# Gate parts brought to the scores' left factor by DMA, first choice's marks in PSUM, constants two units earlier

## The chip, the cores and the metric

The kernel runs on one core of one Trainium2 chip. The metric is the device time of one execution in microseconds (us). Beside the median of three runs there is one profiled execution, from which all rows below come. Engine names in rows: PE is TensorE's matmul, PEld its weight load, DVE VectorE, ACT ScalarE, POOL GpSimd, and SPq the queue of SyncE, which issues nearly all transfers here.

## The reference

A recurrent attention, then a mixture of experts with a capacity, then a dense MLP. The change touches the attention and the first step of the assignment.

```python
for t in range(S):                       # q, k, v: 4 batches x 8 heads x 768 x 40
    m_new = np.maximum(f[t] + m, i[t])
    f_stab, i_stab = np.exp(f[t] + m - m_new), np.exp(i[t] - m_new)
    C = f_stab * C + i_stab * outer(v[t], k[t]); n = f_stab * n + i_stab * k[t]
    y[t] = sigmoid(o[t]) * (C @ q[t]) / np.maximum(abs(n @ q[t]), 1.0)
logits = x @ w_gate                      # 3072 tokens x 8 experts, from the reshaped y
# tokens go to experts in order of falling logit, at most 384 to one expert
out = expert MLP of each token's expert, then a dense MLP of all tokens
```

## The kernel before

The sequence is cut into 9 chunks of 86 steps (`NCH`, `L`). A unit is one chunk `c` of one batch `b` with its 8 heads; the loop in `attention` runs over 36 units `u`, and `score(u)` runs two units ahead of `value(u)`. Within a chunk the recurrence is a matrix of scores: `pS` is keys by queries, `W` is the exponential of a sum of gate terms, `dk` their product, and `pY` the product of `dk` with the values.

The exponent is itself a matmul. `pE` = `cE`^T `aE`: the gate sums of a key position (`cp`, its input part) and those of a query position (`ap`) are each split into three bfloat16 parts, and `cE` (left factor) and `aE` (right factor) hold these parts beside constant rows of ones, of an identity and of the mask. There are three buffers of each, used in turn by `c % 3`. `gates` computes `cp` and `ap` with one partition for each of the 32 pairs, which lie (batch, head): partition 8b + h. Its three generators cover chunk 0, chunks 1 to 3 and chunks 4 to 8.

- `load_a(c)` brings `ap` to three rows of `aE` with three DMAs, for chunk c + 2 in the unit with b = 3 of chunk c, behind `load_qk` and `load_k` of that chunk in the same queue.
- `gates_rows(c)` brings `cp` to 24 rows of `cE`: 12 matmuls with a 0/1 matrix `sel` put the parts into PSUM (`pc`), ScalarE copies them to `cE`. It is called in the unit with b = 2, for chunk c + 1.

In the code's order SP's queue gets, per chunk: in b = 2 `load_v(c + 2)` and `load_o(c + 1)`; in b = 3 `load_qk` (two `q`, one `k`), `load_k` (`kr`), `load_a` (three `aE`); in each unit from u = 8 on the next half of the dense MLP's 64-bit weights (`words`, tile `r`), which `float32_of` turns into float32 on ACT, DVE and POOL, one half in two units up to u = 23 and one in each from u = 24; and in each unit the store `xd` of unit u - 2. `rows` splits loads and stores of 86 rows into 80 and 6.

`first_choice` finds each token's best expert from transposed logits, at units 25 (four chunks), 33 (three), 37 and at the end (one each): the logits `lg` lie in the PSUM tile `pT` (32 columns for a token, 8 of them used), the marks `ch` in the SBUF tile `fc`. `constants` is a generator of eight steps, `cst`: ten small loads on SP in the first three, then small tables by GpSimd and VectorE. One step is taken per unit from u = 28:

```python
if u >= 28:
    next(cst, None)
```

After the loop come `store_logits`, the assignment (`rounds`) beside the rest of the conversion, and the MLPs; nothing in them is touched.

Of the kernel before, what the change touches and what calls it, by code (L numbers as in the profile page):

```python
# [9 lines left out]
F32 = mybir.dt.float32  # L10
F32R = mybir.dt.float32r
BF = mybir.dt.bfloat16
# [4 lines left out]
OP = mybir.AluOpType  # L17
AX = mybir.AxisListType

B, H, S, D = 4, 8, 768, 40  # L20
DM = H * D
N = B * S
E = 8
CAP = N // E
L = 86
NCH = 9
SP = L * NCH
X = D + L
KE = 27 + L
# [8 lines left out]
OUT = 1.0e38  # L38
# [22 lines left out]
def host_constants():  # L61
    import ml_dtypes
    bf = ml_dtypes.bfloat16
    ce = np.zeros((KE, X), np.float32)
    ce[24:27, :] = 1.0
    ce[27:, :L] = np.eye(L)
    ae = np.zeros((KE, H, L), np.float32)
    for p in range(3):
        for h in range(H):
            ae[p * 8 + h, h, :] = 1.0  # L70
    ae[27:] = np.where(np.arange(L)[:, None] > np.arange(L)[None, :], -1e30, 0.0)[:, None, :]
    sel = np.zeros((32, B, 3, 24), np.float32)
    for b in range(B):
        for p in range(3):
            for h in range(H):
                sel[8 * b + h, b, p, 8 * p + h] = 1.0
    g = np.arange(128)
    return {
        "c_blk": (g[:, None] // 16 == g[None, :] // 16).astype(bf),
        "c_pre": ((g[:, None] // 16 == g[None, :] // 16) & (g[:, None] < g[None, :])).astype(bf),  # L80
        "c_tri": (g[:, None] < g[None, :]).astype(bf),
        "c_sel": sel.astype(bf),
        **steps(""), **steps("_a"),
        "c_ce": np.pad(ce, ((0, 128 - KE), (0, 0))).astype(bf),
        "c_ae": np.pad(ae.reshape(KE, H * L), ((0, 128 - KE), (0, 0))).astype(bf),
    }


def host_layout(inp):
    q, k, v = inp["q"], inp["k"], inp["v"]  # L90
    o = {}

    def chunks(a):
        p = np.zeros((B, H, SP, a.shape[-1]), np.float32)
        p[:, :, :S] = a
        return p.reshape(B, H, NCH, L, a.shape[-1])

    def dmajor(a):
        a = chunks(a).reshape(B, 4, 2, NCH, L, D).transpose(3, 2, 5, 0, 1, 4)
        return np.ascontiguousarray(a).reshape(NCH, 2, D, 16, L)  # L100

    def rows(a):
        return np.ascontiguousarray(chunks(a).transpose(2, 3, 0, 1, 4))

    o["h_q"] = dmajor(q)
    o["h_kt"] = dmajor(k).reshape(NCH, 2 * D, 16, L)
    o["h_kr"] = rows(k).reshape(NCH, L, 32, D)
    ve = np.ones((NCH, L, 32, D + 1), np.float32)
    ve[..., :D] = rows(v).reshape(NCH, L, 32, D)
    o["h_v"] = ve  # L110
    o["h_o"] = rows(inp["o_gate"]).reshape(NCH, L, B, DM)
    o["h_i"] = np.ascontiguousarray(inp["i_gate"].reshape(32, S))
    o["h_f"] = np.ascontiguousarray(inp["f_gate"].reshape(32, S))
    wg = np.zeros((128, 3, 32), np.float32)
    for d in range(3):
        n = min(128, DM - 128 * d)
        wg[:n, d, :E] = inp["moe_w_gate"][128 * d:128 * d + n]
    o["h_wg"] = wg

    def dblocks(w):  # L120
        f = w.shape[-1] // 128
        a = np.concatenate([w[..., :DM, :], w[..., 256:DM, :]], axis=-2)
        a = a.reshape(w.shape[:-2] + (3, 128, f, 128))
        return np.moveaxis(a, (-4, -3, -2, -1), (-2, -3, -4, -1))

    we = np.empty((E, FE, 128, 2, 384), np.float32)
    we[:, :, :, 0] = dblocks(inp["moe_w1"]).reshape(E, FE, 128, 384)
    w2 = inp["moe_w2"].reshape(E, FE, 128, DM)
    we[:, :, :, 1, :64] = w2[..., 256:]
    we[:, :, :, 1, 64:] = w2  # L130
    o["h_we"] = we.reshape(E, FE, 128, 768)
    wf = np.empty((NF, 128, 384 + DM), np.int64)
    wf[:, :, :384] = dblocks(np.ascontiguousarray(inp["moe2_w_in"]).view(np.int64)).reshape(NF, 128, 384)
    wf[:, :, 384:] = np.ascontiguousarray(inp["moe2_w_out"]).view(np.int64).reshape(NF, 128, DM)
    o["h_wf"] = wf
    o["h_al"] = np.ascontiguousarray(inp["moe2_alpha"].reshape(NF, 128).T)
    o.update(host_constants())
    return o

# [20 lines left out]
class Kern:  # L160
# [80 lines left out]
    def gates_setup(self, p):  # L241
        nc, a = self.nc, self.a
        self.gp = p
        P = 32
        self.fg = self.cst.tile([P, SP], F32, name="fg", tag="g_fg")
        self.ig = self.cst.tile([P, SP], F32, name="ig", tag="g_ig")
        nc.sync.dma_start(self.fg[:, :S], a["h_f"])
        nc.scalar.dma_start(self.ig[:, :S], a["h_i"])
        ce0 = p.tile([128, X], BF, name="ce0")
        ae0 = p.tile([128, H * L], BF, name="ae0")  # L250
        self.sel = p.tile([32, B, 3, 24], BF, name="sel")
        nc.sync.dma_start(ae0, a["c_ae"])
        nc.scalar.dma_start(ce0, a["c_ce"])
        nc.scalar.dma_start(self.sel, a["c_sel"])
        self.keep = p.tile([P, NCH, L], F32, name="keep", tag="keep")
        self.m = self.cst.tile([P, SP], F32, name="gm", tag="g_m")
        self.cum = self.cst.tile([P, SP], F32, name="cum", tag="g_cum")
        self.cp = p.tile([P, 3, SP], BF, name="cp")
        self.ap = p.tile([P, 3, SP], BF, name="ap")
        self.cE = [p.tile([KE, B, X], BF, name=f"cE{r}") for r in range(3)]  # L260
        self.aE = [p.tile([KE, B, H, L], BF, name=f"aE{r}") for r in range(3)]
        self.ce0, self.ae0 = ce0[:KE], ae0[:KE]

    def gates_fill(self):
# [45 lines left out]

    def load_a(self, c, eng):
        for i in range(3):
            eng.dma_start(self.aE[c % 3][24 + i:25 + i], self.ap[:, i, c * L:(c + 1) * L])

    def attention(self):
        nc, a, tc = self.nc, self.a, self.tc
        with ExitStack() as ctx:
            p = self.pool("at", ctx=ctx)
            w = self.pool("atw", bufs=2, ctx=ctx)
            ps = self.pool("aps", space=bass.MemoryType.PSUM, ctx=ctx)  # L320
# [49 lines left out]
                rows(OG[c], a["h_o"][c])  # L370

            def fill_a(r):
                nc.vector.tensor_copy(self.aE[r].rearrange("p b h l -> p b (h l)"),
                                      self.ae0[:, None, :].to_broadcast([KE, B, H * L]))

            def fill_c(r):
                nc.vector.tensor_copy(self.cE[r], self.ce0[:, None, :].to_broadcast([KE, B, X]))
# [57 lines left out]
            def score(u):  # L435
                c, b = units[u]
                r = c % R
                W = w.tile([X, H, L], F32, name="W")
                for s in range(2):
                    pE = ps.tile([X, 4 * L], F32, name="pE", bufs=2)  # L440
                    nc.tensor.matmul(pE, self.cE[c % 3][:, b, :], self.aE[c % 3][:, b, 4 * s:4 * s + 4, :],
                                     start=True, stop=True)
                    nc.scalar.activation(W[:, 4 * s:4 * s + 4, :].rearrange("p h l -> p (h l)"), pE, AF.Exp)
                dk = w.tile([X, H, X], F32, name="dk", bufs=3)
                for s in range(2):
                    pS = ps.tile([X, 4, L], F32, name="pS", bufs=2)
                    for j in range(2):
                        nc.tensor.matmul(pS[:, 2 * j:2 * j + 2, :], KT[r][:, 4 * b + 2 * s + j, :],  # L448
                                         Q[r][:, :, 4 * b + 2 * s + j, :], start=True, stop=True)
                    nc.vector.tensor_tensor(dk[:, 4 * s:4 * s + 4, :L], pS, W[:, 4 * s:4 * s + 4, :], op=OP.mult)  # L450
                if c + 1 < NCH:
                    nc.gpsimd.tensor_tensor(dk[:, :, L:], KR[r][:, 8 * b:8 * b + 8, :],
                                            W[:, :, L - 1:L].to_broadcast([X, H, D]), op=OP.mult)
                T[u] = dk
# [31 lines left out]
            def first_choice(c0, n):  # L486

                v = nc.vector
                B3 = [L, n * B, E]
                pT = ps.tile([L, n * B, 32], F32, name="pT", tag="pE", bufs=2)  # L490
# [2 lines left out]
                                        LT[c0 + i], ident)  # L493
                lg = pT[:, :, :E]
                mx = p.tile([L, 4 * B], F32, name="fm")[:, :n * B]
                ch = p.tile([L, 4 * B, E], F32, name="fc")[:, :n * B]
                v.tensor_reduce(mx, lg, axis=AX.X, op=OP.max)
                v.tensor_tensor(ch, lg, mx[:, :, None].to_broadcast(B3), op=OP.is_equal)
                v.tensor_tensor(ch, ch, self.ew[:L, None, :].to_broadcast(B3), op=OP.mult)
                v.tensor_reduce(mx, ch, axis=AX.X, op=OP.max)  # L500
                v.tensor_tensor(ch, ch, mx[:, :, None].to_broadcast(B3), op=OP.is_equal)
                v.tensor_scalar(ch, ch, 0.5, 2 * OUT, op0=OP.subtract, op1=OP.mult)
                lo = max(c0, NCH - 2)
                if c0 < lo:
                    kt = p.tile([L, 4, E, B], F32, name="fk")[:, :n]
# [65 lines left out]
            for u in range(nu + 4):  # L571
                if u < nu:
                    c, b = units[u]
# [2 lines left out]
                        warm_up(u)  # L576
                    if u >= G2:
                        next(g2, None)
                    if b == 2 and c + 1 < NCH:
                        self.gates_rows(c + 1, ps)  # L580
                    if b == 2 and c and c + 2 < NCH:
                        load_v(c + 2)
                    if b == 2 and c and c + 1 < NCH:
# [18 lines left out]
                    logit(NCH - 1, 0, B - 1)  # L602
                if 4 <= u:
                    turn(u - 4)
                if u >= 28:
                    next(cst, None)
                if u == 30:
                    KP = p.tile([L, 3, E, B, 4], F32, name="KP", tag="keep")
# [720 lines left out]
```

## Time and profile before

| | us |
|---|---|
| median of 3 runs (807.00 to 816.62) | 809.03 |
| profiled execution, in all | 807.28 |
| its span, first to last instruction | 805.5 |

| engine | busy us | share of the span |
|---|---|---|
| PE | 722.2 | 90% |
| DVE | 562.3 | 70% |
| ACT | 434.6 | 54% |
| POOL | 422.8 | 52% |

The mean granted TensorE clock is 0.961 of full speed. The shares are means over stages with different limits, so a change in one stage is read from rows of that stage. A wait in the tables below is put down to what ended last before the waiting instruction went on.

### The profile page before, as it was taken

How to read it: one execution, taken by the hardware profiler on the slowest of the kernel's cores; microseconds unless marked ns; L12 is line 12 of the kernel's file. 1: busy time of each engine (PE TensorE's matmuls, PEld its weight loads, DVE VectorE, ACT ScalarE, POOL GpSimd, SP SyncE). 2: the span in 40 equal slices, each digit the busy share in tenths (PEclk: the TensorE clock that was granted, in tenths of full speed). 3: DMA queues.
4: the chain of work that ended last, by engine and by line, in shares of the span. 5: the costliest groups of instructions: out<-in, count | busy, mean ns of one | idle time of the engine just before them, and what ended most of it. 6: DMA issues, size and time to landing. Idle time of an engine off the chain costs nothing.

```text
span 805.5 us, 14932 instructions
## 1 busy us (share of the span) xinstructions
PE 722.2 (90%) x4868; PEld 684.9 (85%) x4868; DVE 562.3 (70%) x2209; ACT 434.6 (54%) x948; POOL 422.8 (52%) x509
## 2 busy tenths in 40 slices
PE   4999999820499999998999999999999999999996
PEld 3999998710388999998999889999999999999996
DVE  7987787888788878767876986797698732322311
ACT  6576656667243572564267346525833664654453
POOL 4565556579462383366149416723941686534133
PEclk9999999955699999999999999999999999999998
DMA  8989889551320140042014004202400343100000
GB/s 190 227 209 229 210 204 228 157 142 43 112 86 1 58 139 26 1 124 98 1 46 151 26 1 123 83 18 68 129 25 1 114 143 104 40 1 25 1 1 25
DMA packets 47530, 72.73 MB, mean 90 GB/s; under 512 B 26096, under 2 KB 30192, under 8 KB 47452
## 3 DMA queue, kind: packets, MB, share of 16 engines
q1 hardware_dynamic: 44332, 62.90, 29.1%
q0 software_dynamic: 2688, 8.65, 3.4%
q8 instruction: 38, 0.62, 0.3%
q14 instruction: 40, 0.33, 0.1%
q10 hardware_dynamic: 432, 0.22, 0.1%
HBM read 62.19 MB, written 9.34 MB: 89 GB/s over the span
## 4 chain that ended last, share of the span: by engine, by line
PE 49%; DVE 14%; POOL 9%; issue 8%; ACT 5%; DMA 2%; SPq 0%; POOLq 0%; DVEq 0%; ACTq 0%
PE ph L1027 23%; PE acc L1027 11%; PE fo L1027 10%; POOL gl L1164 4%; DVE scr L155 3%; DVE rb L155 2%; PE pY L464 2%; POOL wt L1003 2%; DVE g L155 2%; POOL w_dt_float32r L960 1%; ACT m L1157 1%; PE pS L448 1%; ACT gh L1163 1%; POOL w_dt_float L931 1%; ACT m L1156 1%
## 5 line engine op out<-in xcount | busy, mean ns | idle before, releaser
L1164 POOL TENSOR_TENSOR gl<-g,gh 128x384 fp32r<-128x384 f32 x127 | 128.1, 1014 | 226.6 <-ACT gh L1163 218.2
L1003 POOL TENSOR_TENSOR wt<-raw,wt 128x384 fp32r<-128x384 f32 (+1 forms) x128 | 118.1, 942 | 33.1 <-ACT wt L1002 33.0
L1027 PE MATMUL ph<-yh,wfh 128*128 128x384 f32 x384 | 132.9, 346 | 0.0
L1027 PE MATMUL ph<-yh,w_dt_float32r 128*128 128x384 f32 x360 | 122.5, 340 | 0.0
L1027 PE MATMUL fo<-wfh,gh 128*128 128x320 f32 x384 | 116.1, 312 | 0.0
L1163 ACT ACTIVATE gh<-g 128x384 fp32r<-128x384 f32 x127 | 66.0, 523 | 91.0 <-DVE g L155 90.9
L155 DVE SCALAR_TENSOR_TENSOR g<-ph,m 128x384 f32<-128x384 f32 x128 | 70.4, 555 | 61.6 <-ACT m L1157 54.2
L1027 PE MATMUL fo<-w_dt_float32r,gh 128*128 128x320 f32 x360 | 109.9, 314 | 0.0
L1027 PE MATMUL ph<-xh,wt 128*128 128x384 f32 x384 | 100.6, 346 | 0.6 <-ACT xh L1058 0.6
L1089 ACT ACTIVATE hh<-ph 128x384 fp32r<-128x384 f32 x64 | 31.4, 491 | 116.0 <-PE ph L1027 89.6
L1027 PE MATMUL acc<-hh,wt 128*128 128x384 f32 x320 | 88.6, 341 | 0.0
L1027 PE MATMUL ph<-yl,wfh 128*128 128x384 f32 x256 | 84.1, 339 | 0.0
L1027 PE MATMUL fo<-wfh,gl 128*128 128x320 f32 x384 | 80.3, 313 | 0.9 <-POOL gl L1164 0.9
L1157 ACT ACTIVATE m<-m,al 128x384 f32<-128x384 f32 x119 | 73.4, 617 | 3.9
L1156 ACT ACTIVATE m<-ph 128x384 f32<-128x384 f32 x119 | 57.4, 482 | 33.0 <-PE ph L1027 32.0
L1027 PEld LDWEIGHTS ph<-yh,wfh 128*128 128x128 f32 x384 | 72.4, 189 | 0.7 <-issue 0.3
L1027 PEld LDWEIGHTS fo<-wfh,gh 128*128 128x128 f32 x384 | 72.3, 188 | 0.5 <-ACT gh L1163 0.3
L1027 PEld LDWEIGHTS ph<-xh,wt 128*128 128x128 f32 x384 | 69.7, 191 | 1.0 <-ACT xh L1058 0.8
L1002 ACT ACTIVATE wt<-raw 128x384 fp32r<-128x384 f32 x128 | 62.9, 514 | 13.4 <-DMA raw<-in_h_we_dram 13.3
L1027 PEld LDWEIGHTS fo<-w_dt_float32r,gh 128*128 128x128 f32 x360 | 67.9, 189 | 1.3 <-issue 1.3
L1027 PEld LDWEIGHTS ph<-yh,w_dt_float32r 128*128 128x128 f32 x360 | 67.9, 189 | 0.7 <-issue 0.7
L1027 PE MATMUL acc<-hl,wt 128*128 128x384 f32 x192 | 66.6, 347 | 1.0 <-DVE hl L155 1.0
(240 smaller groups left out, 1626.6 us busy)
## 6 DMA issues: line engine op xcount, KB each, us to landing
raw<-in_h_we_dram SPq DMA_DIRECT2D x64, 384.0 KB
r<-in_h_wf_dram SPq DMA_DIRECT2D x32, 352.0 KB
xd<-x SPq DMA_DIRECT2D x36, 120.0 KB
q<-in_h_q_dram SPq DMA_DIRECT2D x18, 215.0 KB
k<-in_h_kt_dram SPq DMA_DIRECT2D x9, 430.0 KB
v<-in_h_v_dram SPq DMA_DIRECT2D x9, 410.0 KB
og<-in_h_o_dram SPq DMA_DIRECT2D x9, 400.0 KB
kr<-in_h_kr_dram SPq DMA_DIRECT2D x8, 400.0 KB
```

What stands on the lines that cost most here:

```text
L155: return f(out, *args, **kw)
L448: nc.tensor.matmul(pS[:, 2 * j:2 * j + 2, :], KT[r][:, 4 * b + 2 * s + j, :], Q[r][:, :, 4 * b + 2 * s + j, :], start=True, stop=True)
L464: nc.tensor.matmul(pY[:M, h, :], dk[:, h, :M], V[c % RV][:, 8 * b + h, :], start=True, stop=True)
L931: nc.gpsimd.tensor_tensor(w, w, sg, op=OP.mult)
L1002: nc.scalar.activation(w[:, :384], r, AF.Copy)
L1003: nc.gpsimd.tensor_tensor(w[:, 384:], r[:, :n], w[:, :n].bitcast(F32), op=OP.subtract)
L1027: self.nc.tensor.matmul(out, w, x, **kw)
L1089: nc.scalar.activation(hh, ph, AF.Relu)
L1156: nc.scalar.activation(m, ph, AF.Relu, scale=-1.0)
L1157: nc.scalar.activation(m, m, AF.Copy, scale=alpha)
L1163: nc.scalar.activation(gh, g, AF.Copy)
L1164: nc.gpsimd.tensor_tensor(gl, g, gh.bitcast(F32), op=OP.subtract)
```

## The change

The 32 pairs lie (head, batch): partition 4h + b. The host lays `i_gate` and `f_gate` out that way, and `aE` has its heads outside its batches. For chunks 1 to 8 `load_a` brings `cp` to `cE` as well, with one DMA per part (32 partitions to 8 partitions of 4 batches), each behind the DMA of the same part for `aE`; the call of `gates_rows` in the loop goes, and chunk 0 keeps its own. In `first_choice` the marks lie in columns 8 to 15 of `pT`, and only the last step writes them to SBUF. `cst` is dealt from u = 26.

```diff
-                sel[8 * b + h, b, p, 8 * p + h] = 1.0
+                sel[B * h + b, b, p, 8 * p + h] = 1.0
...
-    o["h_i"] = np.ascontiguousarray(inp["i_gate"].reshape(32, S))
-    o["h_f"] = np.ascontiguousarray(inp["f_gate"].reshape(32, S))
+    for n, x in (("h_i", "i_gate"), ("h_f", "f_gate")):
+        o[n] = np.ascontiguousarray(inp[x].reshape(B, H, S).transpose(1, 0, 2)).reshape(32, S)
...
-        self.aE = [p.tile([KE, B, H, L], BF, name=f"aE{r}") for r in range(3)]
+        self.aE = [p.tile([KE, H, B, L], BF, name=f"aE{r}") for r in range(3)]
...
     def load_a(self, c, eng):
         for i in range(3):
-            eng.dma_start(self.aE[c % 3][24 + i:25 + i], self.ap[:, i, c * L:(c + 1) * L])
+            eng.dma_start(self.aE[c % 3][24 + i:25 + i].rearrange("o h b l -> o (h b) l"), self.ap[:, i, c * L:(c + 1) * L])
+            if c:
+                eng.dma_start(self.cE[c % 3][8 * i:8 * i + 8, :, :L], self.cp[:, i, c * L:(c + 1) * L])
...
-                nc.vector.tensor_copy(self.aE[r].rearrange("p b h l -> p b (h l)"),
-                                      self.ae0[:, None, :].to_broadcast([KE, B, H * L]))
+                nc.vector.tensor_copy(self.aE[r], self.ae0.rearrange("p (h l) -> p h l", h=H)[:, :, None, :].to_broadcast([KE, H, B, L]))
...
-                    nc.tensor.matmul(pE, self.cE[c % 3][:, b, :], self.aE[c % 3][:, b, 4 * s:4 * s + 4, :],
+                    nc.tensor.matmul(pE, self.cE[c % 3][:, b, :], self.aE[c % 3][:, 4 * s:4 * s + 4, b, :],
...
-                ch = p.tile([L, 4 * B, E], F32, name="fc")[:, :n * B]
+                ch = pT[:, :, E:2 * E]
...
                 v.tensor_tensor(ch, ch, mx[:, :, None].to_broadcast(B3), op=OP.is_equal)
-                v.tensor_scalar(ch, ch, 0.5, 2 * OUT, op0=OP.subtract, op1=OP.mult)
+                fc = p.tile([L, 4 * B, E], F32, name="fc")[:, :n * B]
+                v.tensor_scalar(fc, ch, 0.5, 2 * OUT, op0=OP.subtract, op1=OP.mult)
+                ch = fc
...
-                    if b == 2 and c + 1 < NCH:
-                        self.gates_rows(c + 1, ps)
...
-                if u >= 28:
+                if u >= 26:
                     next(cst, None)
```

## Rows read from the trace of the kernel before

**Rows 1.** Busy time by stretch (us, busy per engine, PEclk, DMA share, GB/s).

```profile
80.00:100.00 20.00, 19.85 (x198) 18.82 (x197) 14.80 (x43) 13.19 (x35) 11.61 (x18) 1.00 0.91 212
```

**Rows 2.** Chain that ended last, in order of time: start us, us, what.

```profile
96.85 0.56 PE pc L307 x12
97.41 1.88 PE pY L464 x16
99.83 1.17 PE pS L448 x8
101.00 1.70 PE pY L464 x16
...
129.14 0.29 PE pE L441 x2
...
162.44 0.21 DVE KP L510
```

**Rows 3.** Waits of SP's queue, 28 to 134 us: us in total, times, longest.

```profile
SPq L909 <- DMA k<-in_h_kt_dram: 9.5, 5, 2.3
SPq L358 <- DMA v<-in_h_v_dram: 7.2, 5, 2.2
SPq L351 <- DMA kr<-in_h_kr_dram: 4.0, 6, 1.0
...
SPq L351 <- POOL dk L452: 0.8, 2, 0.5
```

**Rows 4.** Timeline of SP's queue: start us, us (issue with waits inside a merged row).

```profile
86.23 0.32 SPq L351 DMA_DIRECT2D v<-in_h_v_dram  x1
...
89.23 2.11 SPq L358 DMA_DIRECT2D q<-in_h_q_dram  x2
...
93.73 1.77 SPq L313 DMA_DIRECT2D aE<-ap  x3
95.61 0.53 SPq L351 DMA_DIRECT2D xd<-x  x1
96.86 0.27 SPq L353 DMA_DIRECT2D xd<-x  x1
99.42 0.36 SPq L909 DMA_DIRECT2D r<-in_h_wf_dram  x1
100.65 0.31 SPq L351 DMA_DIRECT2D xd<-x  x1
...
102.19 0.32 SPq L351 DMA_DIRECT2D v<-in_h_v_dram  x1
```

**Rows 5.** Timeline of PE at the start of chunk 6.

```profile
102.77 0.46 PE L441 MATMUL pE<-aE,cE 113*126 113x344 bf16 x2
```

**Rows 6.** Waits for the words: ACT's total, 0 to 166 us, then its timeline.

```profile
ACT sg L924 <- DMA r<-in_h_wf_dram: 5.5, 4, 2.2
...
119.76 0.53 ACT L924 ACTIVATE sg<-r 128x352 f32<-128x352 f32 x1 [1.92 <-DMA r<-in_h_wf_dram]
```

**Rows 7.** Timeline of SP's queue while the loop warms up.

```profile
14.82 3.58 SPq L313 DMA_DIRECT2D aE<-ap  x3
20.59 0.33 SPq L351 DMA_DIRECT2D kr<-in_h_kr_dram  x1
```

**Rows 8.** Timeline of SP's queue: first and last of ten constants.

```profile
134.04 0.35 SPq L193 DMA_DIRECT2D c_blk<-in_c_blk_dram  x1
...
143.37 0.33 SPq L205 DMA_DIRECT2D most_a<-in_c_most_a_dram  x1
```

**Rows 9.** Timeline of DVE, first choice at unit 33.

```profile
148.95 0.26 DVE L498 TENSOR_TENSOR fc<-pT,fm 86x96 f32<-86x96 f32 x1
149.24 0.70 DVE L499 TENSOR_TENSOR fc<-fc,ew 86x96 f32<-86x96 f32 x1
...
150.26 1.05 DVE L501 TENSOR_TENSOR fc<-fc,fm 86x96 f32<-86x96 f32 x1
```

**Rows 10.** Instructions on tile aE: ns min/median/max, first and last start us.

```profile
L373 DVE COPY aE<-ae x3: 857/865/1366, 6.0 to 21.3; 113x2752 bf16<-113x2752 bf16 x3
```

## Prediction

> **What bounds the kernel now.** I read the busy time by stretch first, to find the stage that the edits touch. All of them lie in the attention loop, whose last VectorE step ends at 162.65 us of the 805.5 us span [rows 2]. There TensorE is busy 19.85 us of 20 at full granted clock, and the DMA engines 0.91 of the time [rows 1]: two resources are near their limit at once, and the question is which of them an edit loads. Nothing in the program that follows (assignment, expert MLP) is changed, so whatever the loop gains or loses is passed to the end once.
>
> The chain of waits shows the TensorE side. A plain unit is the scores' matmuls, the value matmuls and two small groups. In a chunk's third unit there are also the 12 gate-row matmuls, 0.56 us, and the value matmuls behind them take 1.88 instead of 1.70 us [rows 2].
>
> The waits of SP's queue show the other side. Between 28 and 134 us it waits almost only for landings of its own earlier transfers: a word load (`r`) waits for `k` 9.5 us in all, `q` for `v` 7.2 us, a store `xd` for `kr` 4.0 us, while the longest total for an engine is 0.8 us [rows 3]. Counting along the queue, the one waited for is always the eighth before: after `v`, `v'`, `og`, `og'`, `r`, `xd`, `xd'`, `q1` comes `q2`, which waits for `v`; after `k`, `kr`, `kr'`, three `aE`, `xd`, `xd'` comes `r`, which waits for `k` (a prime marks the second, six-row half of a load or store). So SP has eight transfers in flight, and it runs through a chunk at its own pace, from `v` at 86.23 to `v` at 102.19: 15.96 us [rows 4]. TensorE's chunk takes about as long. The compute side is hardly ahead: the parts of `aE` for chunk 6 stand behind `kr`, which has landed at 100.65 when `xd` goes, and the last of them has landed by 102.19, since `v` goes eight places after it; the matmul `pE` that needs them starts at 102.77 [rows 4, 5]. Slack: 0.6 to 2.1 us.
>
> From unit 24 on the loop asks for one half of the words (`r`) per unit, twice the rate before, and from unit 27 on they are late: ScalarE's `sg` starts at 119.76, the moment `r` lands, and it stood idle for such landings 5.5 us in all, 4 times [rows 6]. ScalarE's later work in program order (the exponentials of the next unit) stands behind that wait.
>
> **The change, part by part.** *Gate rows leave TensorE.* Chunks 1 to 8 lose 12 matmuls each. Price by the chain: 0.56 us, and 1.88 - 1.70 = 0.18 us on the value matmuls, 0.74 us a chunk, 5.9 us for eight [rows 2]. ScalarE's copies into `cE` go as well; they are not what a unit waits for. The bound is 0 to 5.9 us, and most of it cannot come through: after the first chunks TensorE would arrive earlier at a `pE` whose left and right factors come by the same queue, where the slack is at most 2.1 us, and from unit 27 the words set the pace whatever TensorE does. I count 0 for it at the end.
>
> *Three more transfers per chunk on SP's queue.* The bytes are small (32 pieces of 172, as for `aE`); what counts is the place in the queue. The issue is 1.77 us for three [rows 4]. I walk chunk 6's stretch with the rule of eight. Now, after `kr'`: three `aE`, `xd`, `xd'`, `r` (99.42, on `k`), `xd` (100.65, on `kr`), three more stores, `v` at 102.19: 1.54 us for four places, 0.385 us each. After: `aE` and `cE` take turns. Their waits fall on `r`, `xd`, `xd'`, `q1`, `q2` and, for the sixth, on `k`; so the sixth goes at 99.4, where `r` went. The next `xd` waits for `kr` and goes at 100.65 as before. Behind it now stand seven issues ahead of `v` (`xd`, `xd'`, `r` and four stores) instead of four: 2.70 us, `v` at 103.35, 1.16 us later. The landings that pace the rest of the chunk (`v` for `q2`, `og` for `kr`, `k` for the sixth) all follow from there, so the chunk's cycle grows by 1.16 us. Chunks 3 to 7 are loaded this way: 5.8 us. Chunk 8 has no `kr`; three places more, 1.2 us. Chunks 1 and 2 are loaded while the loop warms up: the first three issues fall where SP stands idle between the end of the `aE` issues at 18.40 and `kr` at 20.59 [rows 7], the next three don't; 1.8 to 3.5 us for both, and I take 2.5, as `og` and the second chunk's `q` move two sets. Sum: SP is 9.5 us late when the words of units 28 to 33 are due. Bounds: 0, if the waits of [rows 3] swallow the issues; 24 x 0.59 = 14.2 us if every one counts in full.
>
> Who waits: the `pE` of each chunk's first unit (TensorE in order, so scores and value matmuls behind it), and from unit 27 `sg` on ScalarE and the word operations on VectorE, each with the next unit's work behind it. There the slack is zero [rows 6], so the lateness passes in full. The stores `xd` are late too, but the logits are taken from SBUF, and nobody reads `xd` before the gather.
>
> *Constants from unit 26.* Ten transfers, now between 134.04 and 143.70 [rows 8], go two units earlier. Three now stand ahead of chunk 8's `q`; at 0.385 us a place that is 1.2 us for the loads of unit 27, and up to 1.5 us at the last late word. In return the last stores and words find a shorter queue. I take -0.5, with +1.5 and -1 as bounds. The few POOL and VectorE instructions move with it; the tail's waits are not on them.
>
> *First choice's marks in PSUM.* At unit 33 the two products that read both inputs from SBUF take 0.70 and 1.05 us, the comparison of the same size that reads PSUM 0.26 us [rows 9]. With `ch` in PSUM both become like the third: -1.2 us, on the chain, as VectorE's work of the next unit stands behind. Bounds: 0 (if GpSimd's work beside them or the PSUM write sets the time) and -1.3. The same edit at unit 25 stands ahead of the word waits and gives nothing at the end. The bank is held to the end of the function now as well, since the last step reads the logits from it.
>
> *The order (head, batch).* The right factor of `pE` is now read in four runs of 86. The scores' right factor is read in runs of 86 already: 1.17 us for eight instructions of 172 float32 columns, 0.146 us each, as long as one of `pE`'s pair needs for 344 bf16 columns (0.29 us for two) [rows 2]. Runs of 86 leave no gap that shows there, so 0; if `pE` took twice as long, 0.29 us a unit would fall on TensorE, and behind SP's queue most of it would be hidden. The three fills of `aE` copy runs of 86 instead of 688; now 857 to 1366 ns [rows 10]. I take +0.5 us once, the other two lying beside other work; bounds 0 and +1.5.
>
> **Sum.** 9.5 - 1.2 - 0.5 + 0.5 = +8.3 us. On the profiled execution (805.5 us span, 807.28 us in all) that is 815.6 us. The median of the runs shown is 1.75 us above that execution, which would make 817.3. I predict 816 us.
>
> **The rivals.** *A: the small transfers are hidden, faster.* SP waits for much of the loop anyway, and if the added issues fall into those waits without moving `v`, TensorE gains its 2.1 us of slack in the loop, the words give it back or not, and the first choice gives 1.2 us: 804 to 806 us; in full, with 5.9 + 1.3, 800 us. For it: the idle in front of `r`, from 97.1 to 99.4 [rows 4], is longer than the added issues. Against it: that idle ends with `k`'s landing, and the seven issues behind `kr` come after it. It decides if the cycle from `v` to `v` stays under 16 us. The Trainium skill, "DMA: Bandwidth & Descriptors", section "Anatomy of one DMA — SWDGE (gpsimd) path", fits a transfer (on GpSimd's path) as some 2.0 us plus its bytes at 436 GB/s: as an estimate by that, a part of `cE` would land 2 us after its issue, long before use, and the case would be A. In the trace the first `q` is waited for from 89.23 to 95.61, 6.4 us, so the queue ahead of a transfer counts for more than its own cost.
>
> *B: it compounds, slower.* If every issue counts in full and the constants add their 1.5 us, SP is 14.2 + 1.5 = 15.7 us late: 823 us on the profiled execution's basis, 825 on the median's. It needs a wait that I took as shared to be paid twice, as where late words hold ScalarE and late `cE` holds TensorE in the same unit.
>
> *C: the edits cancel.* If words and `cE` are late by only some 3 us, the 2.1 us and 1.2 us offset them: 806 to 810 us.
>
> **How the numbers follow.** Forecast (811 to 820): 0.55. A: 0.23. C: 0.12. B: 0.10. The range that holds 8 in 10 leaves out the far ends of A and B: 803 to 825 us. A difference of 2% is 16 us, about what a measurement of this kernel can tell from no change. Faster by more than that has no mechanism here: 0.02. Slower by more is the upper part of B: 0.06. The rest, 0.92, is within 2%.
>
> **What the profile will show.** If I am right: `v` to `v` on SP's queue at some 17.1 us in place of 15.96; `r` behind a store's wait for `kr`, no more on `k`; `pE` of chunks 4 to 8 waiting for a transfer; ScalarE's waits for `r` well above 5.5 us; the loop's end 8 us later; the two products of the first choice at about 0.26 us; and the stages after it as long as now. If the cycle is below 16 us, the step from places to lateness is wrong, and A or C holds. If the cycle is longer but the loop ends no later, the words were not what bounds the end.

## The result, and the profile after

The changed kernel takes 821.1 us (median of four runs, 820.8 to 839.0) against 809.25 us for the kernel before on the same chip: a ratio of 1.0125, with a 95% interval of 1.0083 to 1.0167, or 6.7 to 13.5 us. Its slowest run was disturbed and is left out of the ratio. The profiled execution took 821.06 us, its span 819.3 us.

In the two profiles all of it is lost in the attention loop. VectorE's last `KP`, for chunk 8, ends at 180.47 us; in the kernel before it ends at 166.09 (the `KP` of [rows 2] is chunk 7's, which the prediction took for the last). From there to the end of the span it is 639.4 us before and 638.8 us after. So the loop ends 14.4 us later, and the rest is as long as it was.

Busy time by stretch, after, the columns as in [rows 1]:

```profile
80.00:100.00 20.00, 17.84 (x137) 17.07 (x136) 11.82 (x34) 8.67 (x23) 8.92 (x14) 0.78 0.86 202
120.00:140.00 20.00, 15.70 (x116) 14.63 (x116) 12.79 (x36) 8.23 (x22) 8.01 (x12) 0.72 0.83 186
```

Against [rows 1], TensorE issues 137 matmuls in the same 20 us instead of 198 and is granted 0.78 of full speed instead of all of it; the DMA engines are less busy too, 0.86 instead of 0.91. No engine has more work than before: TensorE does less of it at a lower clock, and the others are less busy. What comes later is SP's queue. Its timeline in the changed kernel, for the loads of chunk 7, which answer to [rows 4] (one line is one issue here, `q` apart):

```profile
93.69 0.32 SPq L353 DMA_DIRECT2D v<-in_h_v_dram  x1
...
96.54 2.06 SPq L360 DMA_DIRECT2D q<-in_h_q_dram  x2
98.91 0.61 SPq L361 DMA_DIRECT2D k<-in_h_kt_dram  x1
100.72 0.32 SPq L353 DMA_DIRECT2D kr<-in_h_kr_dram  x1
...
101.92 0.54 SPq L313 DMA_DIRECT2D aE<-ap  x1
102.50 0.73 SPq L315 DMA_DIRECT2D cE<-cp  x1
...
107.42 0.72 SPq L315 DMA_DIRECT2D cE<-cp  x1
108.79 0.33 SPq L353 DMA_DIRECT2D xd<-x  x1
...
109.60 0.44 SPq L910 DMA_DIRECT2D r<-in_h_wf_dram  x1
...
111.79 0.32 SPq L353 DMA_DIRECT2D v<-in_h_v_dram  x1
```

From `v` to `v` it is 18.10 us; it was 15.96 [rows 4]. The parts, with those of before in brackets: `v` to `k` 5.22 (5.16); `k` to the issue that waits for its landing, now the third `cE`, 8.51 (8.03); from there to the `xd` that waits for `kr` 1.37 (1.23); from that `xd` to `v`, seven issues instead of four, 3.00 (1.54). The order is the one that the prediction walked through; the last part came out dearer. This cycle is among those that grew most: from `v` of chunk 3 to `v` of chunk 8 the five cycles grew by 0.1 to 2.3 us, by 1.51 us in the mean (16.25 to 17.75).

What follows from it, in the waits of SP's queue from 28 to 134 us, of ScalarE to 181 us and of TensorE from 28 to 134 us, which answer to [rows 3] and [rows 6]:

```profile
SPq L315 <- DMA k<-in_h_kt_dram: 9.0, 5, 2.1
```

```profile
ACT sg L925 <- DMA r<-in_h_wf_dram: 12.0, 5, 6.2
```

```profile
PE pE L442 <- DMA cE<-cp: 4.4, 3, 2.0
```

SP waits for `k` as long as before: `k` releases the third `cE` now, no longer `r`. ScalarE waits for words 12.0 us instead of 5.5 [rows 6], and TensorE now waits for `cE`.

The chain that ended last, after, with its start, its length and what it is:

```profile
128.06 3.16 DMA r<-in_h_wf_dram
131.30 0.52 ACT sg L925
...
133.33 1.51 PE pS L449 x4
134.84 3.27 PE pY L465 x16
138.10 1.02 PE pL L567 x24
139.12 0.62 PE pX L553 x3
139.75 0.57 PE pE L442 x2
140.32 2.19 PE pS L449 x8
142.51 1.69 PE pY L465 x16
...
145.57 0.05 ACT w_dt_float L931
145.63 3.30 DMA r<-in_h_wf_dram
149.01 0.53 ACT sg L925
...
149.68 3.48 DMA r<-in_h_wf_dram
```

Here it runs from word to word, as the prediction expected. What it did not expect stands between the words: the value matmuls `pY` take 3.27 us at 134.84 and 1.69 us at 142.51, the same sixteen. In the first case TensorE, after the idle time that the late word left (2.81 us), is at the lower of its two clock levels (1.2 of 2.4 GHz): the granted clock is 0.50 from 133 to 142 us. The next load of a word starts at 145.63, and the chain puts it down to ScalarE's work behind that unit. But SP's own queue was busy until then: from 140.53 to 145.51 it issues `aE` and `cE` one behind the other, and of its waits from 133 to 146 us only 1.0 us is put down to engines, 4.6 us to landings. So a faster unit would have brought this word only a little sooner.

The first choice at unit 33, on VectorE's timeline after, answers to [rows 9]:

```profile
164.54 0.26 DVE L499 TENSOR_TENSOR pT<-pT,fm 86x96 f32<-86x96 f32 x1
164.84 0.26 DVE L500 TENSOR_TENSOR pT<-pT,ew 86x96 f32<-86x96 f32 x1
...
165.42 0.26 DVE L502 TENSOR_TENSOR pT<-pT,fm 86x96 f32<-86x96 f32 x1
...
180.26 0.20 DVE L513 TENSOR_TENSOR KP<-fc,pT 86x32 f32<-86x32 f32 x1
```

The two products take 0.26 us each, as predicted, instead of 0.70 and 1.05.

### The profile page after: what moved, and what is told of

The parts are those of the page before. It is cut to its first block, busy times and chain, and to the rows that moved or that the text cites. A ratio compares the mean times of both kernels' runs of the same rounds, so it can differ in the third digit from the quotient of the medians.

```text
span 819.3 us, 14757 instructions
## 1 busy us (share of the span) xinstructions
PE 729.6 (89%) x4772; PEld 694.5 (85%) x4772; DVE 562.5 (69%) x2209; ACT 431.9 (53%) x940; POOL 422.2 (52%) x509
## 4 chain that ended last, share of the span: by engine, by line
PE 54%; DVE 14%; POOL 8%; issue 7%; ACT 5%; DMA 4%; SPq 0%; POOLq 0%; DVEq 0%; ACTq 0%
PE ph L1028 24%; PE fo L1028 11%; PE acc L1028 11%; DVE scr L155 4%; POOL gl L1165 3%; PE pY L465 3%; DVE rb L155 3%; POOL wt L1004 2%; PE pS L449 2%; DMA r<-in_h_wf_dram 2%; DVE g L155 1%; ACT m L1158 1%; DMA k<-in_h_kt_dram 1%; PE rb L722 1%; ACT gh L1164 1%
## 5 line engine op out<-in xcount | busy, mean ns | idle before, releaser
L465 PEld LDWEIGHTS pY<-v,dk 126*126 126x126 f32 (+1 forms) x576 | 71.5, 200 | 0.0
L465 PE MATMUL pY<-v,dk 126*126 126x41 f32 (+1 forms) x576 | 70.2, 285 | 0.0
```

The costliest lines, as they stand in the source:

```text
L465: nc.tensor.matmul(pY[:M, h, :], dk[:, h, :M], V[c % RV][:, 8 * b + h, :], start=True, stop=True)
```

## The experiments

**Theory:** three more transfers per chunk lengthen SP's cycle, words and inputs arrive late, and the work that TensorE saves is worth nothing. **Rivals:** the constants' or the marks' edit makes the loss; the pieces, not the places, cost; TensorE's wait for the late transfers, with its falling clock, makes the loss at the end, and the lateness of the words little of it.

### Which edit makes the loss

The gates alone: the changed kernel with marks in SBUF and constants from unit 28, as before the change (lines against the changed kernel):

```diff
-                if u >= 26:
+                if u >= 28:
...
-                ch = pT[:, :, E:2 * E]
+                ch = p.tile([L, 4 * B, E], F32, name="fc")[:, :n * B]
...
```

> Only the order (head, batch) and cE by DMA; marks in SBUF and constants from unit 28 as before. If the places in SP's queue are the cause, nearly all of the loss is here: 1.2 us above the first experiment, 817 to 820 us, with v to v on SP's queue at 17.5 to 18 us. If the loss came from the other two edits, it stands at the kernel before, 807 to 810 us.

Measured 822.1 us, ratio 1.0159 (1.0133 to 1.0186). This edit alone makes the whole loss.

The constants alone: the changed kernel with them back at unit 28 (the first line of the cut above), and the kernel before with them at 26:

```diff
-                if u >= 28:
+                if u >= 26:
```

> The changed kernel with the constants dealt from unit 28 again. If the ten constants in front of chunk 8's loads are a large part of the loss (q of chunk 8 goes 16.0 us later than before, v just ahead of it only 10.8 us later), the loop ends 3 to 5 us sooner than in the changed kernel: 816 to 818 us. If the constants only trade places, as the prediction had it (-0.5 us for the move), it stays at 820 to 822 us.

> The kernel before with the constants dealt from unit 26 and nothing else. If ten more issues ahead of chunk 8's loads cost by themselves, +2 to +4 us: 811 to 813 us. If they cost only where SP's queue is late already, within 1 us of before: 808 to 810 us.

Measured 823.9 us, ratio 1.0186 (1.0158 to 1.0215), for the first, and 810.9 us, 1.0032 (1.0008 to 1.0055), for the second. The edit costs some 2.6 us in the old queue. In the new one it seems to help (1.0125 with it, 1.0186 without, intervals that just overlap). SP's timeline after shows both sides:

```profile
130.65 0.32 SPq L353 DMA_DIRECT2D v<-in_h_v_dram  x1
...
135.84 0.35 SPq L193 DMA_DIRECT2D c_blk<-in_c_blk_dram  x1
...
137.51 0.43 SPq L193 DMA_DIRECT2D c_tri<-in_c_tri_dram  x1
138.89 0.68 SPq L360 DMA_DIRECT2D q<-in_h_q_dram  x2
```

From `v` to `q` of chunk 8 it is 8.2 us here and 4.3 us with the gates alone; but there the constants stand between the late words instead, and its loop ends at 180.38 us, against 180.47. They trade places with the words; no size can be given to the gain.

The marks alone, on the kernel before:

```diff
-                ch = p.tile([L, 4 * B, E], F32, name="fc")[:, :n * B]
+                ch = pT[:, :, E:2 * E]
...
+                fc = p.tile([L, 4 * B, E], F32, name="fc")[:, :n * B]
...
```

> The kernel before with the first choice's marks in PSUM and nothing else. If the two products wait for their second SBUF input, both fall to about 0.26 us at unit 33 and the loop ends 1.2 us sooner: 807 to 808 us, a ratio of 0.9985. If the PSUM write sets their time, no change: ratio 1.000.

Measured 809.5 us, ratio 1.0004 (0.9978 to 1.0031). VectorE's two products at unit 33 take 0.26 us each in that run too, 1.23 us less than in [rows 9]. At the end the interval reaches from -1.8 to +2.5 us: a gain of 1.2 is not shown and not excluded. In [rows 9] the two products read both inputs from SBUF at 86x96 elements; at 86x32 the same instructions of the kernel before take 0.19 us, as long as those with an input in PSUM, so the two SBUF inputs alone don't explain 0.70 and 1.05 us. What does stays open.

### The places, without the saving, and the saving, without the places

Kernel before with three unread transfers per chunk; the gate matmuls stay:

```diff
             eng.dma_start(self.aE[c % 3][24 + i:25 + i], self.ap[:, i, c * L:(c + 1) * L])
+            if c:
+                eng.dma_start(self.spare[c % 3][8 * i:8 * i + 8], self.cp[:, i, c * L:(c + 1) * L])
...
```

> The kernel before, with its gate matmuls, and behind each of the three input transfers of a chunk (chunks 1 to 8) one transfer more of the same part of the forget gates into a spare tile that nobody reads: the changed kernel's traffic and queue, with nothing waiting for it. If the places in SP's queue make the loss (seven issues behind the keys instead of four, each at its turn): SP's value loads 17.5 to 18 us apart as in the changed kernel (16.0 before), the attention loop 11 to 14 us longer, 819 to 823 us. If the loss comes from what the change does to TensorE (its first matmul of a chunk waits for the late transfer, the granted clock falls to 0.72 to 0.83 of 2.4 GHz in stretches of the loop, and the loop runs slower for that): value loads 16 to 17 us apart, granted clock 1.00 to 120 us, 808 to 813 us. Between them, at the 17.1 us of the prediction's own count of issues, 814 to 817 us: then the clock makes the rest.

Measured 826.0 us, ratio 1.0171 (1.0095 to 1.0248), value loads 16.1 us apart once and then 18.1 to 20.4. Nothing waits for these transfers, and the loss is there. So the places make it, without the saving and without `cE` being late. They do not rule out the third rival, though: the input transfers `aE` stand between them and are late too, and TensorE, which has no such wait in these 106 us of the kernel before, waits for them. Its waits from 28 to 134 us, and a stretch of the loop:

```profile
PE pE L444 <- DMA aE<-ap: 6.8, 4, 3.3
...
140.00:160.00 20.00, 20.00 (x116) 19.06 (x115) 10.09 (x27) 8.58 (x22) 7.70 (x13) 0.51 0.79 186
```

ScalarE waits for words 2.7 us in this run, less than the 5.5 of [rows 6]. In the chain that ended last a word that lands at 133.46 us still makes TensorE wait, 1.65 us; behind it, from 135.55 to 161.15 us, the chain runs on TensorE's own matmuls at the lower clock (0.51 from 140 to 160), and no longer from word to word. (This profile, 828.96 us, is among the longer of the run's four executions, 823.0 to 829.0.)

Kernel before without the gate matmuls of chunks 1 to 8, and with nothing in their place, so that the scores of these chunks lack the key positions' gate sums:

```diff
-                    if b == 2 and c + 1 < NCH:
-                        self.gates_rows(c + 1, ps)
```

> The kernel before without the twelve gate matmuls and their copy for chunks 1 to 8, and without any transfer in their place: the part of cE that comes from the forget gates stays at its fill for these chunks, so the scores lack it. It prices the work saved alone. The prediction counted 0.74 us a chunk, 5.9 us in all, as worth nothing at the end, because the loop goes by the words and SP's queue: then 806 to 810 us, same. If TensorE bounds the loop: 802 to 804 us.

Measured 811.6 us, ratio 1.0011 (0.9968 to 1.0054). The saved work brings nothing that shows at the end: 5.9 us of gain (0.9927) is excluded, 2.6 us is not. Between 28 and 134 us TensorE now waits 3.2 us for `aE`, where it waited for none: it arrives earlier at transfers that come when they came, as the prediction said.

Three unread transfers again, of one row instead of 32:

```diff
-                eng.dma_start(self.spare[c % 3][8 * i:8 * i + 8], self.cp[:, i, c * L:(c + 1) * L])
+                eng.dma_start(self.spare[c % 3][8 * i:8 * i + 1, 0, :], self.cp[:1, i, c * L:(c + 1) * L])
```

> The run with three unread transfers a chunk beside the gate matmuls again (826.0), but each of them moves one row of 172 bytes in place of 32: as many issues and as many turns among the eight, a thirty-second of the pieces. Its issue should be shorter than the 0.72 us of the 32 pieces, near the 0.3 to 0.4 us of the plain loads. If the price is the place (one issue more, and a wait for the landing of the transfer eight before): value loads 17 to 18 us apart, 817 to 824 us. If it is the pieces (96 small ones more a chunk between the keys and the words, and the long issue): value loads 16 to 16.5 us apart, 809 to 813 us.

Measured 822.4 us, ratio 1.0156 (1.0083 to 1.0230). SP's timeline in that run:

```profile
94.05 0.32 SPq L354 DMA_DIRECT2D v<-in_h_v_dram  x1
...
96.92 4.10 SPq L361 DMA_DIRECT2D q<-in_h_q_dram  x2
101.07 0.61 SPq L362 DMA_DIRECT2D k<-in_h_kt_dram  x1
...
107.70 0.61 SPq L316 DMA_DIRECT2D sp<-cp  x1
109.12 0.33 SPq L354 DMA_DIRECT2D xd<-x  x1
...
112.01 0.32 SPq L354 DMA_DIRECT2D v<-in_h_v_dram  x1
```

17.96 us from `v` to `v`, with 172 bytes a transfer. Within the cycle the parts differ from those of the changed kernel: `k` to the issue that it releases is 6.63 us instead of 8.51, and the second `q` waits longer for `v` (4.10 us with both issues, instead of 2.06). The sum is nearly the same: what this cycle saves at one landing it pays at the next. Two readings give its size. By issues, three more of 0.61 to 0.73 us are 1.8 to 2.2 us. By turns, a cycle has 22 transfers before, counted along the timeline, and 25 after, and 15.96 / 22 = 0.73, 18.10 / 25 = 0.72, 17.96 / 25 = 0.72 us. The expected shorter issue of a tiny transfer was wrong (0.61 us), so these runs don't tell the two apart. Over the five cycles the growth is 1.58 us in this run, 2.20 with the full unread transfers and 1.51 in the changed kernel, so both readings lie at the upper end. The loss needs neither the bytes nor the pieces. TensorE waits for `aE` in this run too, 7.9 us in all.

The Trainium skill, "DMA: Bandwidth & Descriptors", section "Anatomy of one DMA — SWDGE (gpsimd) path", fits a transfer (on GpSimd's path) as a fixed time plus its bytes, which the prediction set beside its rival A. The 172-byte run speaks against using it as the price here: three such transfers cost the issuing queue 1.58 us a cycle, though nobody waits for them.

### The same transfers on another queue, and at another place

The gates' three transfers by GpSimd (the rest as with the gates alone):

```diff
-                eng.dma_start(self.cE[c % 3][8 * i:8 * i + 8, :, :L], self.cp[:, i, c * L:(c + 1) * L])
+                self.nc.gpsimd.dma_start(self.cE[c % 3][8 * i:8 * i + 8, :, :L], self.cp[:, i, c * L:(c + 1) * L])
```

> The changed gates alone (marks and constants as before the change), but their three transfers a chunk go by GpSimd's queue, so that SP's queue is the one of the kernel before. If the places in SP's queue make the loss: value loads 15.5 to 16.5 us apart, granted clock 1.00 to 120 us, 806 to 811 us, some 12 us under the same kernel with all on SP (822.1). If it is the landing of the transfers themselves, many small pieces beside the words' traffic: value loads 17.5 us apart and more, 818 to 823 us. What GpSimd pays for the issues (24 of them) stands against its other work: if each costs 1 us of the decay products, up to 4 us are left of the loss.

Measured 818.3 us (814.4 to 826.2), ratio 1.0112 (1.0019 to 1.0204); above the 806 to 811 us expected if the places are the cause, and not told apart at the end from the runs on SP. By its end this run does not support the places. But its loop splits in two. While the loop warms up, chunk 1's first matmul waits 3.6 us for its input transfers (it starts at 28.2 us, and at 26.2 in the kernel before), and the granted clock is 0.74 from 20 to 40 us: chunk 2, which begins at 40.5 us in the kernel before, begins at 46.2. After that TensorE's chunks are as short as the saving promised. Its timeline at the first matmuls of chunks 3 and 4, in this run, then in the kernel before:

```profile
63.50 0.46 PE L442 MATMUL pE<-aE,cE 113*126 113x344 bf16 x2
...
78.23 0.46 PE L442 MATMUL pE<-aE,cE 113*126 113x344 bf16 x2
```

```profile
56.37 0.46 PE L441 MATMUL pE<-aE,cE 113*126 113x344 bf16 x2
...
71.83 0.46 PE L441 MATMUL pE<-aE,cE 113*126 113x344 bf16 x2
```

14.73 us instead of 15.46: 0.73 us less, where the prediction took 0.74 from the chain. SP's value loads behind the warm-up stay 15.4 to 16.7 us apart. With the places elsewhere, TensorE has its saving, and SP's cycle is the old one. What can keep the end late is the warm-up and, from 28 to 134 us, SP's waits for GpSimd's `x`: 8.9 us, against 0.7 in the kernel before. How much each weighs is not separated.

The input transfers `aE` of the kernel before by GpSimd:

```diff
-            eng.dma_start(self.aE[c % 3][24 + i:25 + i], self.ap[:, i, c * L:(c + 1) * L])
+            (self.nc.gpsimd if c else eng).dma_start(self.aE[c % 3][24 + i:25 + i], self.ap[:, i, c * L:(c + 1) * L])
```

> The kernel before with its three input transfers a chunk (chunks 1 to 8) issued by GpSimd: one issue left behind the keys on SP instead of four. If the places in SP's queue are what sets the chunk's cycle: value loads 14.5 to 15.5 us apart, the loop 4 to 9 us shorter, 800 to 805 us. If the cycle is set elsewhere (TensorE, 19 to 20 of 20 us busy in the loop's first stretches) and only more places would lengthen it: 806 to 810 us, same.

Measured 809.6 us, ratio 0.9991 (0.9949 to 1.0033): same. Fewer places on SP bring nothing at the end.

The six small transfers of chunks 5 to 8 dealt over three units, with the changed gates and with the old ones:

```diff
-                    if b == 3 and c and c + 2 < NCH:
+                    if b == 3 and 0 < c < 3:
                         self.load_a(c + 2, nc.sync)
+                    if b < 3 and c > 2 and c + 2 < NCH:
+                        self.load_a(c + 2, nc.sync, [b])
...
```

> The changed gates alone (marks and constants as before the change), but for chunks 5 to 8 the six small transfers don't go together behind the keys: two go with each of the first three units of the chunk two ahead of their use. As many issues and places in SP's queue as in the changed kernel; only where they stand is changed. If a place costs the same wherever it stands (about 0.4 us for the issue and its turn among eight): value loads 17.5 to 18 us apart in the later chunks too, 819 to 823 us. If the price comes from their standing behind the key load, where they hold places until the keys have landed, and from what is then late behind them: value loads 16 to 17 us apart from the fourth cycle on, 810 to 815 us (what the chunks 3 and 4 lose, 3 to 5 us, stays).

> The same spreading of the three input transfers of chunks 5 to 8, done to the kernel before, with its gate matmuls. If SP's queue alone sets its cycle of 16 us: value loads 15 to 15.5 us apart, 804 to 807 us. If TensorE sets it too (the chunks' first matmuls lie 15.4 to 15.5 us apart in the kernel before, and were as far apart with the three transfers on GpSimd, where SP had time to spare): 807 to 811 us, same.

Measured 822.1 us, ratio 1.0156 (1.0096 to 1.0217), and 812.2 us, 1.0027 (0.9996 to 1.0058). Spread over the units, the later value loads are 16.9 to 17.4 us apart, a little less than in the changed kernel, but the cycle in which the spreading begins takes 21.1 us, and the end is the same. The place in the order matters little at the end; how much of that is the transition, the run doesn't tell. With the old gates there is no gain either. That run's TensorE timeline has the clearest fall of the clock:

```profile
116.75 1.85 PE L464 MATMUL pY<-v,dk 126*126 126x41 f32 x16
...
122.18 1.21 PE L448 MATMUL pS<-q,k 128*126 128x172 f32 x4 [2.16 <-ACT KL L520]
123.18 3.48 PE L464 MATMUL pY<-v,dk 126*126 126x41 f32 x16
...
138.66 3.63 PE L464 MATMUL pY<-v,dk 126*126 126x41 f32 x16
```

TensorE waits 2.16 us once, for ScalarE, and then its sixteen value matmuls take 3.5 us instead of 1.85 until past 142 us, over three units and more. In the kernel before the same wait is 0.89 us and the clock stays at 2.4 GHz. SP is hardly late in this run: its last `v` goes at 120.77 us (119.88 before) and its last `k` at 128.07 (125.68). Yet the loop ends at 175.50 us, 9.4 us later, in a profiled execution of 815.1 us. Its chain runs on TensorE at the lower clock from 122.18 to 147.80 us. So a fall of the clock can cost the loop 9 us where the queue is hardly late.

The version that the runs point to: old gates to chunk 3, and from chunk 4 on the new ones, with all six transfers by GpSimd.

```diff
-            eng.dma_start(self.aE[c % 3][24 + i:25 + i].rearrange("o h b l -> o (h b) l"), self.ap[:, i, c * L:(c + 1) * L])
-            if c:
-                eng.dma_start(self.cE[c % 3][8 * i:8 * i + 8, :, :L], self.cp[:, i, c * L:(c + 1) * L])
+            (self.nc.gpsimd if c >= 4 else eng).dma_start(self.aE[c % 3][24 + i:25 + i].rearrange("o h b l -> o (h b) l"), self.ap[:, i, c * L:(c + 1) * L])
+            if c >= 4:
+                self.nc.gpsimd.dma_start(self.cE[c % 3][8 * i:8 * i + 8, :, :L], self.cp[:, i, c * L:(c + 1) * L])
...
+                    if b == 2 and c + 1 < 4:
+                        self.gates_rows(c + 1, ps)
...
```

> Kernel before for chunks 1 to 3 (gate matmuls, transfers on SP); from chunk 4 on no gate matmuls, and all six small transfers by GpSimd, so that SP issues none of them. It takes both bounds down at once, behind the warm-up in which GpSimd's issues were dear in the two runs before (a first cycle of 21 to 22 us against 17). If the loop is held by TensorE and SP's queue together, at 15.5 and 16.0 us a chunk: chunks 14.7 to 15.2 us apart, 4 to 5 of them shorter by 0.5 to 1 us, 803 to 807 us. If the words' own transfers or GpSimd's six issues (0.55 us each, 3.3 us a chunk, ahead of decay products) hold it: 808 to 813 us.

Measured 810.3 us, ratio 0.9987 (0.9949 to 1.0025): the whole loss is gone, and no gain over the kernel before can be measured. SP's timeline in that run:

```profile
87.62 0.32 SPq L353 DMA_DIRECT2D v<-in_h_v_dram  x1
...
101.96 0.32 SPq L353 DMA_DIRECT2D v<-in_h_v_dram  x1
```

14.34 us and 19 transfers from `v` to `v`, the granted clock 1.00 up to 160 us, the loop's end at 164.6 us against 166.1 in the kernel before. It beats the changed kernel by some 11 us, and not the one before. SP has three places fewer a cycle here than in the kernel before, not only three fewer than in the changed one.

## Why the prediction was right, and where it was off

- **Direction: right, and its cause shown.** The three transfers make the loss without any of the work that the change saves, and with 172 bytes each; with the input transfers beside them on GpSimd's queue from chunk 4 on there is none. The forecast of +8.3 us lies inside the measured 6.7 to 13.5; the median, 821.1 us, lies just above the forecast's own 811 to 820 and inside the whole range.
- **TensorE's saving, counted at 0: right.** It is 0.73 us a chunk, near the 0.74 read from the chain, and without the gate matmuls no gain shows.
- **The chunk's cycle: the term that was mis-sized.** "1.16 us later" was 2.14 us in the cycle shown and 1.51 us in the mean of the five. The step that failed was to move only the issues behind `kr`, at 0.385 us each, and to let the landings stand where they stood. In the cycle shown seven issues took 0.43 us each (3.00 us, against 2.70), `xd` left 0.14 us later behind the one that `k` releases, and that one 0.48 us later. Better prices were already in [rows 4]: an issue of `aE` at 0.59 us, the upper bound's, makes 1.77 us for three, and a cycle's mean of 0.73 us a transfer 2.2 us. The measured cycles lie around the first.
- **Lateness.** The warm-up's +2.5 came as +3.2. At `v` of chunk 8 SP is 10.8 us late (119.88 to 130.65); the sum predicted for that point is 2.5 + 5 x 1.16 = 8.3. At its `k` it is 14.2 us late, the constants included, and the loop ends 14.4 us later in the profile.
- **"The lateness passes in full", by the words: in part.** That SP's lateness reaches the end is right. By which way it does is not settled. In the changed kernel's profile the end of the chain goes by the words; with the unread transfers it goes for 25 us by TensorE at the lower clock; and with the old gates spread the loop ends 9.4 us later though SP's last loads are only 0.9 to 2.4 us late. The prediction had late factors and late words as waits, but no term for the clock. On the changed kernel's chain the four groups from 133.33 to 139.75 take 6.42 us; like groups at the upper clock take 0.85 + 1.69 + 0.58 + 0.38 = 3.50 us in the kernel before. What of this comes through to the end is open, since SP's queue was busy meanwhile; no run held the clock up with the queue as it is.
- **What the runs' clocks say of it.** The kernel before, timed beside the unread transfers, took 806.0 to 807.7 us in its three runs at a mean granted clock of 0.961, and 814.6 to 816.0 us in its three at 0.949. So the same code loses 8 us together with its clock. The changed kernel's runs of 820.8 to 821.1 us come at 0.943 to 0.947: a good part of its loss goes along with the clock. The unread transfers of one row took 822.4 us at 0.949, 6 to 8 us more than the kernel before at that clock: a part does not. Which of the two brings the other, these means don't tell.
- **Marks.** The two instructions fell as predicted, by 1.23 us. The -1.2 us at the end is not seen.
- **Constants.** -0.5 with +1.5 as a bound: alone they cost 2.6 us (0.6 to 4.4), the wrong sign, and by the median beyond the bound. In the full queue their sign is not settled.
- **The order (head, batch) and the fills.** With the gates by GpSimd TensorE's chunk shrank by about what the gate rows took, so reading the factor in runs of 86 costs nothing that shows. The fills' +0.5 us was not measured by itself; the three take 857 to 1016 ns after, against 857 to 1366 [rows 10].
- **Rivals.** A needed a cycle under 16 us; it is 18.10 in the cycle shown, and A fell with the unread transfers. Its counter-argument had a misreading: no wait of SP ends at 95.61 in [rows 4]; the one that does, for the second `q` (issued at 91.05), ends at 96.86, 5.8 us after the issue, so the argument stands with that number. C needs lateness of 3 us; it was 10.8. B's premise was that every issue counts in full, 0.59 us; the mean of the five cycles, 1.51 / 3 = 0.50 us a transfer, lies between that and the 0.385 us. B's sum (823) lies above the profiled 821.06.

## What to carry to other kernels

A queue that always waits for the landing of its own earlier transfers has no free places: price an added transfer by its place and not by its bytes, and don't hold the landings still while moving the issues. Here the price was 0.50 us in the mean of five cycles and 0.71 us in the one shown, more than the 0.385 us of the issues that the prediction counted. Unread transfers show the price of the places alone, but look at what stands between them: here they made TensorE's own inputs late. Work taken off an engine brings nothing while another queue has the same cycle; here TensorE (15.5 us) and SP (16.0 us) were level, and taking down either alone, or both from chunk 4 on, moved the end by less than could be measured. Moving a tiny transfer to another engine's queue is worth trying where that engine is not late, and not during the warm-up.

## What the runs showed of the hardware

- A transfer of 172 bytes from SBUF to SBUF occupied SP for 0.61 us, one of 32 such pieces for 0.72 us; a load of 410 KB from DRAM, 0.32 us. The time of an issue does not go by the bytes.
- A wait of about 2 us on TensorE was followed by the lower clock level for 6 us in the changed kernel and for 24 us in the run with the old gates spread, but not each time: in the run with one-row transfers TensorE waits 2.13 us before 110.32, and the granted clock is 1.00 from 100 to 120 us. In the changed kernel, TensorE's timeline:

```profile
46.42 1.27 PE L449 MATMUL pS<-q,k 128*126 128x172 f32 x4 [1.96 <-DVE LT L570]
47.48 3.47 PE L465 MATMUL pY<-v,dk 126*126 126x41 f32 x16
...
53.82 1.85 PE L465 MATMUL pY<-v,dk 126*126 126x41 f32 x16
```

The same sixteen matmuls take 3.47 and, one unit later, 1.85 us. Here a wait of 1.96 us was followed by a unit of nearly twice the length. When a queue is made later, look for the stretches in which TensorE's granted clock falls, and not only for the waits.
